# A recurrent attention and a squared-ReLU layer on one core: attention in two stretches of small products, and three passes summed in one bank

## The chip, the core and the metric

The kernel runs on one core of a Trainium2 chip. Five engines work side by side, each from its own queue in order: TensorE (PE in the profile: matrix products into PSUM, with its weight loads shown as PEld), VectorE (DVE), ScalarE (ACT), GpSimd (POOL) and SyncE (SP), which here issues all DMA transfers. PSUM has eight banks of 128 partitions x 512 fp32 values; a sum of products builds up in one bank and is read from there by VectorE or ScalarE. The metric is the device time of one execution in microseconds.

## What is computed

```python
# q, k, v, alpha: (4, 8, 768, 48); batch, heads, sequence, head size
for t in range(S):
    state = alpha[:, :, t, :, None] * state + einsum('bhd,bhe->bhde', k[:, :, t], v[:, :, t])
    y[:, :, t] = einsum('bhd,bhde->bhe', q[:, :, t], state)
x = y.transpose(0, 2, 1, 3).reshape(3072, 384)
h = maximum(x @ w_in, 0.0)          # w_in  (384, 2048)
out = h * h @ w_out                 # w_out (2048, 384)
```

All in fp32; the weights arrive as 64-bit floats and are converted on the chip.

## The kernel before

**Blocks, groups, pairs.** The sequence is cut into chunks of 128 positions; one chunk of one batch entry is a block (24 in all, numbered chunk first). Four blocks are a group (512 tokens; six groups, 0 to 5). Attention is worked on in pairs of blocks, the dense layers in groups. While TensorE does the dense layers of group g, the attention of group g + 1 is threaded between their products.

**Attention of a pair.** Logarithms of alpha (`pair_ln`) are summed along the chunk by a product with a triangle of ones (`cs`), and their exponentials scale k and q (`eb`, `ei`, `pair_mk`, `pair_mq`). Then come four kinds of small products, which use 64 rows of the array each so that several run at a time: `turn` (L672) transposes k and q in halves of 64 positions (16 transposes a block, 64 rows by 128 columns) into two banks, and `turned_copied` (L686) copies them to SBUF; `pair_scores` (L545, 64 products into two banks) multiplies k and q of the same half, and `pair_masked` on VectorE (L563) copies the causal part out; `pair_sums` (L569, up to 64 products into two banks) multiplies k and v; `pair_states` (L587) adds these to the running state in three VectorE instructions (L596, L603, L604); and `y_first`, `y_second` (L623, L640, 96 and 32 products into two banks) make the output. `y_second` writes from the other half of the rows into banks that `y_first` has written, and so its first product waits for an instruction on POOL's queue (L636) that itself waits for the end of `y_first`. `ev` (L697, L714) copies y to the place of the next layer's input.

**Where these stand.** `PLAN` (L1155) gives offsets in units of dense work, `attention` (L1172) turns them into events, and `weave` (L1213) emits every event that is due before the next unit. A unit of 1 is about 1.3 us of TensorE. For a step with start t, `turn` of both new blocks stands at one place, `ga` at a second and `gb` at a third. `ga` (L653) emits the scores and masks of pair n and `y_first` of the pair before it; `gb` (L662) emits the sums of pair n, `y_second` of the pair before, and the states of n. The numbers in `AT` (L19) set all starts, due times, split sizes and the engines of some copies. The work on the first four blocks is written out by hand in the string `first` (L1139); there k and q are transposed by 128x128 transposes (`turned`, L416).

**Dense layers in three passes.** From group 1 on, a product x w is made of parts that TensorE multiplies at its faster fp32r rate. With E = 2^-12, x = a / E + l and w = E (b + lw), where a and b are rounded to fp32r. Then

x w = (1 + E) (a b + l lw) + (a - l)(lw - E b).

`split_to` (L808) makes a on ScalarE (L809) and l on VectorE (L810); `diff_to` (L814) makes a - l on VectorE (recorded at L747). The weights' parts are made by `cast_w`, `rest_w` and `diff_w` (L759 to L791), stored to DRAM and streamed back from there in each group; `room` caps how many tiles of them are asked for at a time, in a pool of 25 buffers. Per piece j of 128 of the 2048 columns, `in_x` (L842) does the first two passes into one bank; then the factor is applied in one of two ways, by the letter in `kinds` for j modulo 4. With "D", ScalarE copies E times the bank to SBUF (L849), the third pass is added to the same bank (`in_y`, L853), VectorE adds the copy (L856, recorded at L747) and then takes maximum and square in one instruction (L863). With "A", ScalarE multiplies the bank in place (L851), the third pass is added, and ScalarE does ReLU and square (L868, L872). The third pass follows `lag` pieces behind, the activation `post` pieces behind. `layer_in` lists these units.

**The second layer** works the same way on h * h (`split_h`, `diff_h`, three parts a piece). In groups 2 to 4 the output is made transposed (`turned_x`, `turned_y`, L993 and L1009), with ScalarE multiplying the bank in place between the passes (L1005) and VectorE transposing it at the end (L1022). Group 5 and the last k1 of the eight weight pieces in group 1 (k0 in group 0) use `out_x` and `out_y` (L941, L965); between the passes E times the bank goes to or into the output tile (L956, L961), and VectorE adds the bank at the end (L979, recorded at L747). The other pieces of groups 0 and 1 use plain fp32 products (`out_plain`, L929), which leave two TensorE records each. The first layer of group 0 is plain too (`ffn_in`, L1083).

Of the kernel before, what the change touches and what calls it, by code (L numbers as in the profile page):

```python
# [9 lines left out]
FP32 = mybir.dt.float32  # L10
# [3 lines left out]
ALU = mybir.AluOpType  # L14
# [4 lines left out]
AT = {'pad': 1, 'lag': 2, 'joined': 0, 'tc': 0.02, 'u0': 2, 'evs': 0.55, 'lead': 6, 'post': 2, 'w_first': (38.96, 41.47, 110.86), 'wstep': 2.64, 'w_in_at': 0.78, 'w_in_by': 3.53, 'room1': 24, 'room': 27, 's0': 3, 'ahead': 12, 'late': 23, 'xs': 0.23, 'g0': (3.39, 20.49, 26.97), 'sc0': (2.38, 2.19, 2.43), 'g1': (3.89, 18.11, 27.72), 'g': (3.4, 16.07), 'g1x': 51.78, 'gx': 47.62, 'g0x': 56.0, 'k0': 2, 'h0': 15, 'k1': 5, 'h1': 1, 'h1by': 1, 'evs0': 0.17, 'tp': 'DDAD', 'tp1': 'AADD', 'split': 8, 'o0': (41.33, 43.5), 'o1': (), 'o2': (18.91, 14.16, 27.32, 25.44, 44.09, 46.91), 'str1': 19.63, 'ga': 9.84, 'gb': 13.76, 'osb': 'DD', 'hia': 16}  # L19
# [6 lines left out]
def kernel(  # L26
# [406 lines left out]
    VECTOR = ('k0', )  # L433
# [6 lines left out]
    def qc(n):  # L440
        (copied if n < GB else turned_copied)("q", n)

    def kc(n):
        (copied if n < GB else turned_copied)("k", n)
# [203 lines left out]
    def turn_and_copy(m):  # L648
        turn(m)
        kc(m)  # L650
        qc(m)
# [34 lines left out]
    def turned_copied(x, n):  # L686
        t = blk[n][f"{x}s"] = work(f"{x}s", 2 if x == "k" else 4)
        for h in range(2):
            nc.scalar.copy(out=t[:, :, HALF[h]], in_=blk[n]["T"][h][:, "kq".index(x)])
# [40 lines left out]
    NEAR = 1.0 - 2.0**-13  # L730
    acc = {}
# [47 lines left out]
    def diff_w(w, p):  # L779
# [4 lines left out]
            out=d, in0=b, scalar=-E, in1=l, op0=ALU.mult, op1=ALU.add  # L784
# [29 lines left out]
    def diff_to(d, a, l):  # L814
        combine(((d, a.bitcast(FP32), ALU.subtract, l.bitcast(FP32)),))
# [11 lines left out]
    def diff_x(g):  # L827
        x_parts["d"] = raw_r("xd")
        diff_to(*(flat(x_parts[k]) for k in "dal"))
# [12 lines left out]
    def in_x(j):  # L842
        acc["h", j] = ps_ffn.tile([128, GB * C], FP32, tag="att", name="h")
        in_passes(j, "b", "a", True, False)
        in_passes(j, "l", "l", False, True)
        x = acc["h", j]
        if kinds[0][j % 4] == "D":
            hid[j] = two_k("hid")
            nc.scalar.activation(out=hid[j], in_=x, func=AF.Copy, scale=E)  # L849
        else:  # L850
            nc.scalar.activation(out=x, in_=x, func=AF.Copy, scale=1.0 + E)  # L851
# [6 lines left out]
    kinds = [""]  # L858

    def in_post(j):  # L860
        if kinds[0][j % 4] == "D":
            h = hid[j]
            nc.vector.scalar_tensor_tensor(  # L863
                out=h, in0=h, scalar=0.0, in1=h, op0=ALU.max, op1=ALU.mult
            )
            return
        h = hid[j] = two_k("hid")
        nc.scalar.activation(out=h, in_=acc.pop(("h", j)), func=AF.Relu)  # L868
        if kinds[0][j % 4] == "M":
            combine(((h, h, ALU.mult, h),))  # L870
        else:
            nc.scalar.activation(out=h, in_=h, func=AF.Square)  # L872
# [20 lines left out]
    def split_h(n, i):  # L893
# [8 lines left out]
        split_to(a, l, hid.pop(n))  # L902
        h_parts[n] = a, l

    def diff_h(n):
        h_diff[n] = two_k("hd", FP32R)
        diff_to(h_diff[n], *h_parts[n])
# [33 lines left out]
    def out_x(n, first, g):  # L941
        p, jj = divmod(n, 2)
        a, l = h_parts.pop(n)
        for t in range(GB):
# [3 lines left out]
            of_tile(t, l, mixed(here["l", "o", p], jj), stop=n == NJ - 1)  # L948
            if n == NJ - 1:
                x = unmixed(acc[t])  # L950
                if first and AT["osb"][g] == "A":
                    x = acc[t][:, 0:DM]
                    nc.scalar.activation(out=x, in_=x, func=AF.Copy, scale=1.0 + E)
                elif first:
                    o = out_tile(t).rearrange("a (q c) -> a q c", c=DM // 128)
                    nc.vector.scalar_tensor_tensor(  # L956
                        out=o, in0=x, scalar=E, in1=o, op0=ALU.mult, op1=ALU.add
                    )
                else:
                    o = new_out(t).rearrange("a (q c) -> a q c", c=DM // 128)  # L960
                    nc.scalar.activation(out=o, in_=x, func=AF.Copy, scale=E)  # L961
# [3 lines left out]
    def out_y(g, ps, t, last):  # L965
# [5 lines left out]
        if last:  # L971
            o = out_tile(t)
# [3 lines left out]
            for i in range(parts):  # L976
                qs = slice(i * 128 // parts, (i + 1) * 128 // parts)
                cols = slice(i * DM // parts, (i + 1) * DM // parts)
                combine(((o[:, qs], x[:, qs], ALU.add, o[:, qs]),))  # L979
# [7 lines left out]
    TURNED = (2, 3, 4)  # L987
# [5 lines left out]
    def turned_x(n):  # L993
        p, jj = divmod(n, 2)
        a, l = h_parts.pop(n)
        for c in range(NM):
            if n == 0:
                acc[c] = ps_ffn.tile([128, GB * C], FP32, tag="att", name="o")
            for w, x in (("b", a), ("l", l)):
                nc.tensor.matmul(  # L1000
                    out=acc[c], lhsT=by_parts(here[w, "o", p], jj, c), rhs=x,
                    start=n == 0 and w == "b", stop=n == NJ - 1 and w == "l", skip_group_check=True,
                )
            if n == NJ - 1:
                nc.scalar.activation(out=acc[c], in_=acc[c], func=AF.Copy, scale=1.0 + E)  # L1005
# [77 lines left out]
    def ffn_in(g, j, cols=slice(0, GB * C)):  # L1083
# [14 lines left out]
        nc.scalar.activation(out=hid[j][:, cols], in_=r, func=AF.Square)  # L1098
# [34 lines left out]
    for x in "stky":  # L1133
# [6 lines left out]
        load1v warm0 warm0 load0v ln0 cs0 ln1 warm0 ei0 eb0 cs1 warm0 mq0 mk0 load2a  # L1140
        weights0 qT0 load3a kT0 eb1 mq1 ei1 warm0 mk1 kc0 qc0 kT1 qT1 kc1 sc0 qc1 kv0 sc1
        lt1 ln2 load2k cs2 am1 load2q lc1 kv1 gt1 am0 warm0 ln3 load3q warm0 us0 cs3 ei2
        first0 us1 ya0 yb0 lt0 eb2 eb3 ei3 st1 mk2 mq2 ea00 load3k kT2 kc2 warm0 lc0 load2v
        mq3 qT2 ed02 gy0 weights1 load3v middle0 lt2 st0 lt3 mk3 qT3 kT3 warm0 warm0 lc2
        qc2 sc2 kc3 qc3 ed01 second0 first1 ea03 load4q middle1 kv2 load4k weights2 am2 us2
        sc3 kv3 am3 us3 gk3 lc3 load4a second1 ha0 weights3 ya2 yb2 ea20 ed21 ed22 ha1 ed23
        first2 middle2 ha3 st3 ha2 load4v hb1 hb0 weights4 st2
    """
    for word in first.split():
# [6 lines left out]
        (-0.48, "pair_ln"),  # L1156
        (-0.27, "pair_sp"),
        (2.08, "cs0 cs1 eb0 ei0"),
        (2.23, "eb1 ei1"),
        (3.01, "pair_bl"),  # L1160
        (3.13, "pair_mk"),
        (4.43, "pair_mq"),
        (5.99, "pair_br"),
        (6.75, "turn"),
        (7.02, "kc0 qc0"),
        (7.36, "kc1 qc1"),
        (9.56, "ga"),
        (10.29, "gb"),
    )
    JOINED = AT["joined"]  # L1170

    def attention(pairs, scale):  # L1172

        out = []
        for t, n0, after, *last in pairs:
# [146 lines left out]
```

## Time and profile before

| what | value |
|---|---|
| three timed runs | 514.6, 513.85, 514.68 us (median 514.6) |
| profiled execution, its own time | 514.06 us |
| its span | 512.3 us |
| TensorE clock granted | 1.00 throughout |
| TensorE products busy | 505.1 us, 5164 records |
| VectorE busy | 371.5 us, 550 instructions |
| ScalarE busy | 304.3 us, 611 instructions |
| DMA | 102.72 MB, mean 201 GB/s |
| dense layers of groups 1, 2, 3, 4, 5 begin at | 123.8, 210.8, 289.4, 368.0, 442.6 us |
| last product ends | 508.6 us |

Times in the profile count from the start of the span, which is a little shorter than the device time. A row of a group gives line, engine, operation, output and inputs, shape, count, busy time and mean duration of one; behind the second bar stands how long the engine was idle just before these instructions and which instruction ended most of that. Products overlap in the array, so that the starts of records, and not their durations, tell how fast TensorE goes on. The chain of waits is followed back from the last instruction, at each step to what released it.

### The profile page before, as it was taken

To read this page: it belongs to the slowest core of one execution; us is meant where nothing else is said; L and a number is where in the kernel's file an instruction comes from. 1 tells how busy PE (TensorE), PEld (TensorE's weight loads), DVE (VectorE), ACT (ScalarE), POOL (GpSimd) and SP (SyncE) were. 2 spreads that over 40 slices of the span, in tenths; PEclk is the share of its full clock that TensorE was granted. 3 is DMA by queue.
4 is the path that set the end of the run, shared out by engine and by line. 5 is a ranking of instruction groups with operands and counts; after the bars stand their busy time and mean duration, and the time that the engine had idled before them with its cause. 6 is when DMAs were issued, how large, how long until landed. Compare 5 with 4: busy or idle time off the path is not lost.

```text
span 512.3 us, 12578 instructions
## 1 busy us (share of the span) xinstructions
PE 505.1 (99%) x5164; PEld 402.5 (79%) x5164; DVE 371.5 (73%) x550; ACT 304.3 (59%) x611; POOL 5.6 (1%) x27
## 2 busy tenths in 40 slices
PE   8999999999999999999999999999999999999997
PEld 6684456669887679988888888888888888888996
DVE  3898879978879957687795388694477685466951
ACT  4689893766988586375863165954165863154520
POOL 4000000000000000000000000000000000000000
PEclk9999999999999999999999999999999999999999
DMA  9999669254978886896877877876874645889201
GB/s 185 217 268 263 196 170 260 51 154 151 289 225 233 217 175 170 291 332 181 177 202 210 275 219 189 185 216 167 267 215 135 201 113 146 276 282 363 91 1 63
DMA packets 144521, 102.72 MB, mean 201 GB/s; under 512 B 116296, under 2 KB 117960, under 8 KB 144464
## 3 DMA queue, kind: packets, MB, share of 16 engines
q1 hardware_dynamic: 144464, 101.91, 70.8%
q8 instruction: 41, 0.67, 0.5%
q14 instruction: 16, 0.13, 0.1%
HBM read 84.57 MB, written 17.33 MB: 199 GB/s over the span
## 4 chain that ended last, share of the span: by engine, by line
PE 94%; DVE 2%; SPq 2%; DMA 1%; issue 0%; ACT 0%; DVEq 0%; POOLq 0%
PE h L834 33%; PE o L913 22%; PE o L1000 13%; PE h L1090 8%; PE o L1012 6%; PE y L465 5%; PE T L681 2%; PE sc L553 2%; PE kv L580 2%; SPq L134 2%; DMA a_lent<-in_alpha_dram 1%; PE cs L327 1%; PE cs L330 1%; PE cs L331 1%; DVE am L494 0%
## 5 line engine op out<-in xcount | busy, mean ns | idle before, releaser
L849 ACT ACTIVATE hid<-h 128x512 f32<-128x512 f32 x56 | 33.3, 595 | 66.2 <-PE h L834 65.6
L834 PE MATMUL h<-xa,wb 128*128 128x512 f32 x240 | 67.7, 391 | 0.0
L834 PE MATMUL h<-xl,wl 128*128 128x512 f32 x240 | 67.6, 390 | 0.0
L834 PE MATMUL h<-xd,wd 128*128 128x512 f32 x240 | 67.5, 396 | 0.0
L714 ACT COPY x<-y 32x256 f32<-32x256 f32 (+2 forms) x137 | 48.6, 366 | 22.8 <-PE y L465 20.5
L747 DVE TENSOR_TENSOR hid<-h,hid 128x512 f32<-128x512 f32 x56 | 38.6, 689 | 28.0 <-PE h L834 25.4
L834 PEld LDWEIGHTS h<-xl,wl 128*128 128x128 f32 x240 | 45.1, 188 | 9.6
L834 PEld LDWEIGHTS h<-xa,wb 128*128 128x128 f32 x240 | 44.9, 188 | 9.5
L834 PEld LDWEIGHTS h<-xd,wd 128*128 128x128 f32 x240 | 44.0, 188 | 8.9
L913 PE MATMUL o<-w_out,hid 128*128 128x384 f32 x144 | 49.0, 492 | 0.0
L1090 PE MATMUL h<-x,w_in 128*128 128x512 f32 (+1 forms) x120 | 42.4, 509 | 0.0
L863 DVE SCALAR_TENSOR_TENSOR hid<-hid 128x512 f32<-128x512 f32 x56 | 38.7, 692 | 1.8
L913 PEld LDWEIGHTS o<-w_out,hid 128*128 128x128 f32 x144 | 26.6, 190 | 17.0
L809 ACT ACTIVATE ha<-hid 128x512 fp32r<-128x512 f32 x42 | 26.2, 638 | 19.1 <-DVE hx L810 11.7
L1090 PEld LDWEIGHTS h<-x,w_in 128*128 128x128 f32 x120 | 22.6, 190 | 17.2 <-issue 14.6
L810 DVE SCALAR_TENSOR_TENSOR hl<-ha,hid 128x512 fp32r<-128x512 f32 x42 | 28.8, 686 | 7.4 <-ACT ha L809 7.3
L1012 PE MATMUL o<-hd,wd 128*128 128x512 f32 x144 | 33.4, 391 | 0.0
L1012 PEld LDWEIGHTS o<-hd,wd 128*128 128x128 f32 x144 | 26.8, 188 | 6.1 <-ACT o L1005 0.6
L747 DVE TENSOR_TENSOR hd<-ha,hl 128x512 fp32r<-128x512 f32 x42 | 29.1, 692 | 2.4
L810 DVE SCALAR_TENSOR_TENSOR hx<-hx,hid 128x512 fp32r<-128x512 f32 x36 | 24.7, 685 | 7.9 <-ACT hx L809 7.9
L851 ACT ACTIVATE h<-h 128x512 f32<-128x512 f32 x24 | 14.0, 584 | 24.7 <-PE h L834 24.6
L1000 PE MATMUL o<-hx,wb 128*128 128x512 f32 x72 | 28.4, 394 | 0.0
(135 smaller groups left out, 945.8 us busy)
## 6 DMA issues: line engine op xcount, KB each, us to landing
wd<-do SPq DMA_DIRECT2D x37, 384.0 KB, 4.2
wl<-lo SPq DMA_DIRECT2D x34, 384.0 KB, 3.8
wl<-li SPq DMA_DIRECT2D x32, 384.0 KB, 4.4
wd<-di SPq DMA_DIRECT2D x32, 384.0 KB, 5.8
raw<-in_moe_w_in_dram SPq DMA_DIRECT2D x8, 768.0 KB
raw<-in_moe_w_out_dram SPq DMA_DIRECT2D x8, 768.0 KB
v_in<-in_v_dram SPq DMA_DIRECT2D x24, 192.0 KB, 3.8
a_in<-in_alpha_dram SPq DMA_DIRECT2D x22, 192.0 KB, 4.0
```

The source lines that it names most:

```text
L465: ins = nc.tensor.matmul(out=ys[e][64 * half : 64 * half + D + G * e, m % 2, p // 2, t], lhsT=lhsT, rhs=rhs, start=(half, e) not in seen, ...
L714: copy(out=x[kk][to : to + m, t : t + 2], in_=blk[n]["y"][e][r : r + m, :, p // 2],)
L747: nc.vector.tensor_tensor(out=o, in0=x, in1=z, op=op)
L809: nc.scalar.activation(out=a, in_=x, func=AF.Copy, scale=NEAR * E)
L810: nc.vector.scalar_tensor_tensor(out=l, in0=a.bitcast(FP32), scalar=-1.0 / E, in1=x, op0=ALU.mult, op1=ALU.add)
L834: nc.tensor.matmul(out=acc["h", j], lhsT=here[w, "i", p][:, kk, jj * 128 : (jj + 1) * 128], rhs=x_parts[x][:, kk], start=start and kk == 0 ...
L849: nc.scalar.activation(out=hid[j], in_=x, func=AF.Copy, scale=E)
L863: nc.vector.scalar_tensor_tensor(out=h, in0=h, scalar=0.0, in1=h, op0=ALU.max, op1=ALU.mult)
L913: nc.tensor.matmul(out=acc[t][:, 0:DM], lhsT=lhs[:, t * C : (t + 1) * C], rhs=rhs, start=start, stop=stop, skip_group_check=True,)
L1000: nc.tensor.matmul(out=acc[c], lhsT=by_parts(here[w, "o", p], jj, c), rhs=x, start=n == 0 and w == "b", stop=n == NJ - 1 and w == "l", ski ...
L1012: nc.tensor.matmul(out=acc[c], lhsT=by_parts(here["d", "o", p], n % 2, c), rhs=h_diff[n], start=False, stop=last and n == NJ - 1, skip_gro ...
L1090: nc.tensor.matmul(out=ps, lhsT=w[:, kk, c0 : c0 + 128], rhs=xT[g][kk][:, cols], start=(kk == 0), stop=(kk == KM - 1),)
```

## The change

**Factor.** The third part of x and of h is now made as a - x E / (1 + E), that is E (a - l) / (1 + E), and that of w as (w_l / E - b), so that the third product is 1 / (1 + E) of what it was. All three passes then add up in one bank to x w / (1 + E). The factor 1 + E of the first layer stands in the scale of the ReLU; that of the second layer stands in the square of h. The copies and the multiplications between the passes are gone (L849, L851, L956, L961, L1005), and so is the "D" way. A letter now names only the engine of the square: "V" is VectorE, "A" is ScalarE. Since the difference now reads h itself, h is kept until then. Where a whole output is made by three passes, VectorE copies it from the bank instead of adding.

**Attention.** A step now emits two stretches. `stretch_a` emits, for pair n, scores, masks and sums, then the transposes of the first block of the pair ahead, then the states of n and the copies of what was transposed. `stretch_b` emits `y_first` of the same pair n, the transposes of the second block ahead, `y_second`, and the copies. A step is prepared one pair further ahead, so that group 0 has a first step with transposes alone; loads of k, v and q are issued at the stretches.

**Numbers.** `AT` is new in nearly all entries (among them lag 2 to 1, post 2 to 1, k1 5 to 6, pad 1 to 9, the letters of `kinds`), the hand-written order `first` is permuted, with four of its warm-up products (`warm0`) left out and the engines of two copies of y (`ea03`, `ed02`) swapped, k and q of blocks 1 to 3 are transposed by halves, and VectorE takes the copies of k0, k2, q0, q1 and q2 (k0 alone before).

```diff
-AT = {'pad': 1, 'lag': 2, ... 'room1': 24, 'room': 27, 's0': 3, 'ahead': 12, ... 'k0': 2, 'h0': 15, 'k1': 5, ... 'tp': 'DDAD', 'tp1': 'AADD', ... 'ga': 9.84, 'gb': 13.76, 'osb': 'DD', 'hia': 16}
+AT = {'turned': (2, 3, 4), 'ht': '123', 'vc': ['k0', 'k2', 'q0', 'q1', 'q2'], 'pad': 9, 'lag': 1, ... 'post': 1, ... 'room1': 23, 'room': 25, 's0': 2, 'ahead': 11, ... 'k0': 2, 'h0': 16, 'k1': 6, ... 'tp': 'AVVA', 'tp1': 'AVVV', ... 'ga': 8.09, 'gb': 12.66, 'hia': 8}
...
+        if str(n) in AT["ht"]:
+            if "T" not in blk[n]:
+                blk[n]["T"] = [bank(n, "T", (2, NP, 64)) for _ in range(2)]
+            for p in range(NP):
+                for h in range(2):
+                    marks["t", n] = nc.tensor.transpose(
+                        out=blk[n]["T"][h][:, "kq".index(x), p, :],
+                        in_=rows[HALF[h], 128 * p : 128 * (p + 1)], identity=ident[HALF[h], HALF[h]],
+                    )
+            return
...
-    def ga(a, n, t):
-        if t is not None and JOINED:
-            turn_and_copy(t)
+    def stretch_a(n, t):
         if n is not None:
             pair_scores(n)
             pair_masked(n)
-        if a is not None:
-            y_first(a)
-
-    def gb(a, n, t):
-        if t is not None and JOINED:
-            turn_and_copy(t + 1)
-        if n is not None:
             pair_sums(n)
-        if a is not None:
-            y_second(a)
+        if t is not None:
+            turn(t)
         if n is not None:
             pair_states(n)
+        if t is not None:
+            kc(t)
+            qc(t)
+
+    def stretch_b(n, t):
+        if n is not None:
+            y_first(n)
+        if t is not None:
+            turn(t + 1)
+        if n is not None:
+            y_second(n)
+        if t is not None:
+            kc(t + 1)
+            qc(t + 1)
...
-            out=d, in0=b, scalar=-E, in1=l, op0=ALU.mult, op1=ALU.add
+            out=d, in0=l, scalar=1.0 / E, in1=b, op0=ALU.mult, op1=ALU.subtract
...
-    def diff_to(d, a, l):
-        combine(((d, a.bitcast(FP32), ALU.subtract, l.bitcast(FP32)),))
+    def diff_to(d, a, x):
+        nc.vector.scalar_tensor_tensor(
+            out=d, in0=x, scalar=-E / WHOLE, in1=a.bitcast(FP32), op0=ALU.mult, op1=ALU.add
+        )
...
-        in_passes(j, "l", "l", False, True)
-        x = acc["h", j]
-        if kinds[0][j % 4] == "D":
-            hid[j] = two_k("hid")
-            nc.scalar.activation(out=hid[j], in_=x, func=AF.Copy, scale=E)
-        else:
-            nc.scalar.activation(out=x, in_=x, func=AF.Copy, scale=1.0 + E)
+        in_passes(j, "l", "l", False, False)
 
     def in_y(j):
         in_passes(j, "d", "d", False, True)
-        if kinds[0][j % 4] == "D":
-            combine(((hid[j], acc.pop(("h", j)), ALU.add, hid[j]),))
+
+    def squared(h, kind, scale):
+        if kind == "V":
+            nc.vector.scalar_tensor_tensor(
+                out=h, in0=h, scalar=scale, in1=h, op0=ALU.mult, op1=ALU.mult
+            )
+        else:
+            nc.scalar.activation(out=h, in_=h, func=AF.Square, scale=scale**0.5)
...
         h = hid[j] = two_k("hid")
-        nc.scalar.activation(out=h, in_=acc.pop(("h", j)), func=AF.Relu)
-        if kinds[0][j % 4] == "M":
-            combine(((h, h, ALU.mult, h),))
-        else:
-            nc.scalar.activation(out=h, in_=h, func=AF.Square)
+        nc.scalar.activation(out=h, in_=acc.pop(("h", j)), func=AF.Relu, scale=WHOLE)
+        squared(h, kinds[0][j % 4], WHOLE if j >= plain_part[0] else 1.0)
...
-            if n == NJ - 1:
-                nc.scalar.activation(out=acc[c], in_=acc[c], func=AF.Copy, scale=1.0 + E)
...
-    steps0 = [(GB, False), (GB + 2, True), (GB + 4, True, True)]
-    if JOINED:
-        steps0.insert(0, (GB - 2, False))
+    steps0 = [(GB - 2, True), (GB,), (GB + 2,)]
```

More of the change, by code (lines that the diff above doesn't have):

```diff
@@ L730 @@
     NEAR = 1.0 - 2.0**-13
+    WHOLE = 1.0 + E
     acc = {}
@@ L947, in out_x @@
             of_tile(t, a, mixed(here["b", "o", p], jj), start=n == first)
-            of_tile(t, l, mixed(here["l", "o", p], jj), stop=n == NJ - 1)
-            if n == NJ - 1:
[L950 to L961, printed above, removed]
+            of_tile(t, l, mixed(here["l", "o", p], jj))
         if jj:
@@ L978, in out_y @@
                 cols = slice(i * DM // parts, (i + 1) * DM // parts)
-                combine(((o[:, qs], x[:, qs], ALU.add, o[:, qs]),))
+                if alone:
+                    nc.vector.tensor_copy(out=o[:, qs], in_=x[:, qs])
+                else:
+                    combine(((o[:, qs], x[:, qs], ALU.add, o[:, qs]),))
                 store(g, t, out_tile(t)[:, cols], cols)
```

123 lines of the change are left out of this document (53 added, 70 removed).

## The prediction

> **What bounds the kernel now.** I read the page's busy shares and chain first, then the chain in order of time, then TensorE's timeline where small products interrupt large ones, then the costliest groups.
>
> ```profile
> PE 505.1 (99%) x5164; PEld 402.5 (79%) x5164; DVE 371.5 (73%) x550; ACT 304.3 (59%) x611; POOL 5.6 (1%) x27
> PE 94%; DVE 2%; SPq 2%; DMA 1%; issue 0%; ACT 0%; DVEq 0%; POOLq 0%
> ```
>
> The chain is TensorE for 94% of the span; in order of time it leaves TensorE only before 30 us (loads, then VectorE) and after 508.6. From 30 us, time is saved only by shortening TensorE's stream, and lost only by making TensorE wait. Around a stretch of transposes (columns: start, us, engine, line, operation, operands):
>
> ```profile
> 138.22 0.84 PE L834 MATMUL h<-xl,wl 128*128 128x512 f32 x3
> 138.99 0.46 PE L681 MATMUL T<-ident,k_in 64*128 64x64 f32 x8
> 139.29 0.42 PE L681 MATMUL T<-ident,q_in 64*128 64x64 f32 x8
> 139.54 0.42 PE L681 MATMUL T<-ident,k_in 64*128 64x64 f32 x8
> 139.79 0.42 PE L681 MATMUL T<-ident,q_in 64*128 64x64 f32 x8
> 140.14 0.98 PE L834 MATMUL h<-xd,wd 128*128 128x512 f32 x3
> 140.96 0.86 PE L834 MATMUL h<-xa,wb 128*128 128x512 f32 x3
> 141.65 0.85 PE L834 MATMUL h<-xl,wl 128*128 128x512 f32 x3
> ```
>
> Read the starts. Undisturbed triples come every 0.685 us. From 138.22 + 0.685 = 138.905 to 141.65 - 2 x 0.685 = 140.28 is 1.375 us for 32 transposes, which run at 0.25 us per 8, so 1.00 us: the visit costs 0.375 beyond its work. The stretch of 64 scores at 144.49 costs 0.315 the same way (1.295 between the large products, less 64 scores in 0.98, the step from 74.05 to 75.03 where sums follow scores). Two more rows show another change of form:
>
> ```profile
> 12.18 0.57 PE L485 MATMUL sckv<-qs,ks 48*64 48x64 f32 x24
> 12.69 0.43 PE L407 MATMUL cs<-ident,b_wide 32*128 32x32 f32 x4
> ```
>
> The last score starts at 12.54 and the first 32-row transpose at 12.69, though scores follow each other at 0.015.
>
> The groups that the change touches on the other engines:
>
> ```profile
> L849 ACT ACTIVATE hid<-h 128x512 f32<-128x512 f32 x56 | 33.3, 595 | 66.2 <-PE h L834 65.6
> L747 DVE TENSOR_TENSOR hid<-h,hid 128x512 f32<-128x512 f32 x56 | 38.6, 689 | 28.0 <-PE h L834 25.4
> L863 DVE SCALAR_TENSOR_TENSOR hid<-hid 128x512 f32<-128x512 f32 x56 | 38.7, 692 | 1.8
> L851 ACT ACTIVATE h<-h 128x512 f32<-128x512 f32 x24 | 14.0, 584 | 24.7 <-PE h L834 24.6
> L1012 PEld LDWEIGHTS o<-hd,wd 128*128 128x128 f32 x144 | 26.8, 188 | 6.1 <-ACT o L1005 0.6
> L872 ACT ACTIVATE hid<-hid 128x512 f32<-128x512 f32 x24 | 15.2, 632 | 0.8
> ```
>
> They wait for TensorE; hardly any of TensorE's idle time is put down to them.
>
> **The change, part by part.** The sum starts from the profiled execution's 514.06 us (span 512.3), 0.54 below the median 514.6 of the three timed runs.
>
> *Factor in the third pass and the ReLU.* Removed: ScalarE 33.3 + 14.0 (L849, L851), 4.7 (L1005), 1.6 (L961); VectorE 38.6 + 38.7 (L747 on hid, L863), 3.9 (L956). Added: 56 more ReLUs x 0.612 = 34.3 and 12 more squares x 0.632 = 7.6 on ScalarE; 44 squares x 0.692 = 30.4 on VectorE. Net ScalarE -12, VectorE -51. All of it lies beside TensorE, so the time gains nothing by it, except the 0.6 that weight loads waited for L1005: **-0.3** (0 to -0.6). The split differences keep one VectorE instruction each (686 for 692 ns). hid now lives until its difference is made, so with 22 buffers the first such difference of the second layer waits for the first out product; TensorE's next three inputs are ready by then, which covers it. The third pass one piece behind instead of two: its ScalarE partner is gone, nothing.
>
> *One more w_out piece in three passes in group 1 (k1 5 to 6).* Sixteen plain records go (4 tiles x 2 halves x 2): 10.52 us for 32 in the chain, so 5.26. Added 24 products, 15.48 us for 88, so 4.22. **-1.04**, all on the path. Preparing it was done anyway; only its kept copies and loads move.
>
> *Fewer stretches.* After 30 us the trace has 33 visits to small products: 10 of transposes, 10 begun by scores, 9 by sums, 4 of y products alone. After the change each of 10 pairs has two, and the first two blocks' transposes, which fall into one unit boundary, add one: 21. Twelve fewer at 0.315 to 0.375: **-4.2** (-3.8 to -4.5).
>
> *New changes of form inside a stretch.* Sums to transposes in the first, y to transposes to y in the second: 27 over nine pairs (the last pair has no transposes). No such pair of neighbours is in the trace. Scores to sums in one form cost nothing seen (one end, 0). Scores to 32-row transposes left 0.149 instead of 0.015, and the transposes' first eight took 0.05 longer (0.30 for 0.25): 0.18 (other end; 4.9 in all). In that row rows and columns both change, here only the columns, so I take two thirds, 0.12: **+3.2**.
>
> *y_second behind y_first.* It waits for a POOL instruction. At 17.12 y products took until 19.03 where 96 at 0.45 per 32 and one change make 1.5: 0.4 of wait. Sixteen transposes (0.50) cover that in the new stretch, except for the last pair: **+0.4** (0 to 0.5).
>
> *Start.* ScalarE's logarithm of blocks 2 and 3 gates the chain until 15.7 (DMA 9.38 + 6.30); the second of those loads goes two places earlier (two loads of 192 KB at the stretch's 213 GB/s: 1.8 us earlier), but both v loads go behind it, and the same 15 loads must land before blocks 2 and 3 are complete. VectorE, which gates the y products at 28.28, gets 1.4 us of copies for block 2 (four at about 0.35 by the halves of L438's 0.69). Eight more pads (0.29 each by L270's pair) lie in the wait for the first load; two warm products are left out there and two further on. **+0.3** (-1.5 to +2).
>
> *Queues.* Loads of q, k and v move to the stretches on SP's queue; each is used more than five units (6 us) later against 3.8 to 4.6 us to landing. The weights' buffers are 25 in both, so lower room numbers start no transfer later. POOL keeps its one instruction per pair. Nothing.
>
> Sum: 514.06 - 0.3 - 1.04 - 4.2 + 3.2 + 0.4 + 0.3 = **512.4 us**.
>
> **Rivals.**
>
> *Inner changes are free:* 512.4 - 3.2 = 509.2, with a better start 508. For it: 48x48, 48x64 and 64x48 products alternate inside y and sums without a gap. Against: every change of form in the trace shows one.
>
> *Inner changes cost the full 0.18:* 512.4 + 1.7 = 514.1, no change. For it: the gap is 0.148 to 0.155 whatever forms meet (scores to 128 rows, 32-row transposes to 128, 64-row transposes to 128). [...]
>
> *TensorE waits for VectorE and banks (slower):* scores, sums and transposes now hold six of eight PSUM banks at once, and two h sums the rest; the next h sum needs a bank 0.68 us after the transposes end, when the masks (1.36 us, begun 1.5 us before that end) must have freed one. That holds while VectorE starts the masks less than about 0.8 us late. Before, it started 0.05 to 3.1 us late (scores end 254.68, mask 257.80). If ten pairs wait 0.45 each: 516.9. Above 0.32 each it is slower. Against: VectorE has 51 us less, and in the second stage of each group the masks now stand ahead of the splits.
>
> *The start loses 2 us:* 514.1 to 514.4.
>
> **How the numbers follow.** Chances: the forecast (511 to 513.4) 0.34; free 0.25; full price 0.17; waits 0.17; start 0.07. 0.2% of the median, 1.03 us, is about what a measurement can tell from no change: faster means under 513.57. Faster: 0.34 + 0.25 and some 0.03 of the last three, 0.62. Same: most of full price and start, 0.18. Slower: waits and the tails, 0.20. The range, 508.6 to 517.0, takes in free and waits to their centres; the forecast's own is 511 to 513.4.
>
> **What would show it.** Twenty-one stretches; the gap from the last sum or y product to the first transpose (0.015, 0.09 or 0.15 us) sets the price. No L849 or L851, 80 ReLUs, 44 squares on VectorE. Second-layer plain records 128. Wrong if waits of TensorE for masks, states or banks reach 3 us in sum, or if large products begin for good more than 1.5 us from 29.96.

## The result, and the profile after

| | before | after |
|---|---|---|
| median (range) of six runs each | 514.64 us (513.85 to 515.99) | 518.82 us (518.61 to 519.17) |
| profiled execution, its own time | 514.06 us | 518.65 us |
| its span | 512.3 us | 516.9 us |
| dense layers begin for good, last product ends | 30.03, 508.59 us | 35.38, 513.32 us |

The ratio is 1.0075, with a 95% interval from 1.0056 to 1.0094. The change made the kernel 4.2 us slower; 512.4 us was forecast, with a range up to 517.0, and the time lies above it. The last row of the table says where to look: the part from the first lasting run of large products to the last product takes 477.94 us instead of 478.56, so it became 0.6 us shorter, but it begins 5.35 us later.

The page of the kernel after (engines' busy time, granted clock, chain by engine, and two groups of other engines):

```profile
PE 510.1 (99%) x5204; PEld 411.2 (80%) x5204; DVE 322.7 (62%) x488; ACT 289.2 (56%) x584; POOL 5.5 (1%) x27
...
PEclk9979999999999999999999999999999999999999
...
PE 98%; DVE 1%; issue 0%; POOL 0%; DVEq 0%; POOLq 0%
...
L876 ACT ACTIVATE hid<-h 128x512 f32<-128x512 f32 x80 | 47.7, 603 | 96.8 <-PE h L848 58.6
L866 DVE SCALAR_TENSOR_TENSOR hid<-hid 128x512 f32<-128x512 f32 x44 | 30.3, 690 | 68.6 <-ACT hid L876 68.5
```

VectorE and ScalarE do less, as forecast, and still wait for TensorE. TensorE's share of the chain rose from 94% to 98%. That looks like a better filled engine; but it lies at the start, where loads led the chain before and TensorE itself leads it now. Of the 4 points (some 20 us), 9.6 us are pads (products of 8 columns ahead of the first attention work) and warm-up products (256 columns), which compute nothing that is read; the rest is attention of the first blocks, part of it at a lower clock: the third slice has a granted clock of 7 tenths. A row of the chain in order of time (columns: start, length, engine, operation and line, count) shows the pads:

```profile
4.02 3.64 PE pad L270 x18
```

And TensorE's timeline, first of before, then of after (start, length, operation; in brackets the idle time just before and what ended it):

```profile
3.81 0.43 PE L270 MATMUL pad<-s 128*128 128x8 f32 x2
4.10 1.50 PE L260 MATMUL warm<-s 128*128 128x256 f32 x4
5.44 0.81 PE L327 MATMUL cs<-a_in,causal 128*128 128x384 f32 x2
...
7.29 0.91 PE L327 MATMUL cs<-a_in,causal 128*128 128x384 f32 x2 [0.61 <-ACT a_in L291]
```

```profile
3.82 3.85 PE L270 MATMUL pad<-s 128*128 128x8 f32 x18
7.52 1.63 PE L327 MATMUL cs<-a_in,causal 128*128 128x384 f32 x2
...
10.64 1.49 PE L327 MATMUL cs<-a_in,causal 128*128 128x384 f32 x2
...
25.71 0.69 PE L425 MATMUL T<-ident,k_in 64*128 64x64 f32 x8 [1.43 <-DVE k_in L358]
```

Look at the first `cs` in the timeline of before: it has no bracket. It waited for nothing but TensorE's own queue, since ScalarE had made its input (L291, 0.52 us from 3.60 on) by 4.12 us. So whatever is put in front of it delays it. After the change the first `cs` is 2.1 us later and the second 3.35 us later, and the products themselves take 1.63 us where they took 0.81: the full clock, granted at 4.91 us before, now comes at 12.08. (These times are from the clock's own records, which begin with that grant; the 1.00 throughout in the table of before holds from there on. Ahead of the grant half clock is read from the starts: the warm-up records of before follow each other by 0.43 us ahead of it and by 0.21 behind it.)

Later TensorE waits 1.43 us for VectorE at 25.71. By the next view (windows of 4 us of the kernel after: window, length, busy time and count of TensorE's products, of its weight loads, of VectorE, ScalarE and POOL, granted clock, DMA share, GB/s) the clock is then halved:

```profile
24.00:28.00 4.00, 2.57 (x50) 1.98 (x48) 3.96 (x8) 0.65 (x2) 0.00 (x0) 0.72 0.73 149
28.00:32.00 4.00, 4.00 (x104) 3.75 (x103) 2.51 (x9) 2.94 (x9) 0.00 (x0) 0.50 1.07 325
```

In the clock's own records it is half from 25.73 to 32.56 us. Before the change it was full in all of these windows. The table of TensorE's waits after the change has three entries, all ahead of the dense work: this one, 1.1 us for POOL at the very start, and 0.5 for VectorE at 13.94. So the slower rival of the prediction, waits for masks and banks, did not occur in this execution.

### The profile page after: what moved, and what is told of

Its sections match the earlier page's. It is cut to its first block, busy times and chain, and to the rows that moved or that the text cites. A ratio compares the mean times of both kernels' runs of the same rounds, so it can differ in the third digit from the quotient of the medians.

```text
span 516.9 us, 12503 instructions
## 1 busy us (share of the span) xinstructions
PE 510.1 (99%) x5204; PEld 411.2 (80%) x5204; DVE 322.7 (62%) x488; ACT 289.2 (56%) x584; POOL 5.5 (1%) x27
## 4 chain that ended last, share of the span: by engine, by line
PE 98%; DVE 1%; issue 0%; POOL 0%; DVEq 0%; POOLq 0%
PE h L848 32%; PE o L918 21%; PE o L996 13%; PE h L1084 8%; PE o L1006 6%; PE y L475 5%; PE T L691 2%; PE sc L563 2%; PE kv L590 2%; PE cs L327 1%; PE warm L260 1%; PE pad L270 1%; PE sckv L522 1%; PE sckv L495 1%; PE cs L330 1%; PE T L425 1%
## 5 line engine op out<-in xcount | busy, mean ns | idle before, releaser
L876 ACT ACTIVATE hid<-h 128x512 f32<-128x512 f32 x80 | 47.7, 603 | 96.8 <-PE h L848 58.6
L866 DVE SCALAR_TENSOR_TENSOR hid<-hid 128x512 f32<-128x512 f32 x44 | 30.3, 690 | 68.6 <-ACT hid L876 68.5
L725 ACT COPY x<-y 32x256 f32<-32x256 f32 (+3 forms) x138 | 50.0, 364 | 4.0 <-DVE x L725 0.8
L918 PE MATMUL o<-w_out,hid 128*128 128x384 f32 x128 | 43.4, 491 | 0.0
L918 PEld LDWEIGHTS o<-w_out,hid 128*128 128x128 f32 x128 | 23.8, 190 | 15.5 <-issue 0.5
L827 DVE SCALAR_TENSOR_TENSOR hd<-hid,ha 128x512 fp32r<-128x512 f32 x42 | 28.7, 684 | 10.7 <-PE o L996 9.7
L700 ACT COPY ks<-T 128x256 f32<-128x256 f32 x44 | 14.2, 375 | 36.6 <-PE T L691 32.7
L822 DVE SCALAR_TENSOR_TENSOR hx<-hx,hid 128x512 fp32r<-128x512 f32 x38 | 26.0, 684 | 6.7 <-ACT hx L821 6.7
L996 PE MATMUL o<-hx,wl 128*128 128x512 f32 x72 | 28.1, 390 | 0.0
```

The source lines that it names most:

```text
L725: copy(out=x[kk][to : to + m, t : t + 2], in_=blk[n]["y"][e][r : r + m, :, p // 2],)
L822: nc.vector.scalar_tensor_tensor(out=l, in0=a.bitcast(FP32), scalar=-1.0 / E, in1=x, op0=ALU.mult, op1=ALU.add)
L827: nc.vector.scalar_tensor_tensor(out=d, in0=x, scalar=-E / WHOLE, in1=a.bitcast(FP32), op0=ALU.mult, op1=ALU.add)
L866: nc.vector.scalar_tensor_tensor(out=h, in0=h, scalar=scale, in1=h, op0=ALU.mult, op1=ALU.mult)
L918: nc.tensor.matmul(out=acc[t][:, 0:DM], lhsT=lhs[:, t * C : (t + 1) * C], rhs=rhs, start=start, stop=stop, skip_group_check=True,)
L996: nc.tensor.matmul(out=acc[c], lhsT=by_parts(here[w, "o", p], jj, c), rhs=x, start=n == 0 and w == "b", stop=False, skip_group_check=True,)
```

## Experiments on the start

Three kernels ask what in the start is late. The first takes the change and puts the start of before in it (the string `first`, one pad, k and q of blocks 1 to 3 transposed whole, `k0` alone on VectorE).

```diff
-AT = {..., 'ht': '123', 'vc': ['k0', 'k2', 'q0', 'q1', 'q2'], 'pad': 9, ...
+AT = {..., 'ht': '', 'vc': ['k0'], 'pad': 1, ...
-        ln0 cs0 ln1 warm0 warm0 ei0 load2a weights0 cs1 eb0 ei1 mk0 mq0 kT0 load3a warm0
...
+        load1v warm0 warm0 load0v ln0 cs0 ln1 warm0 ei0 eb0 cs1 warm0 mq0 mk0 load2a
...
```

> The changed kernel with the start of the kernel before: its hand-written order, one pad, blocks 1 to 3 transposed 128x128, VectorE copying k0 alone. The changed kernel begins its dense work for good at 35.4 us, the kernel before at 30.0. Theory A (the whole loss lies in the start; the dense part gained 0.65 us): dense work from about 30.0, 518.7 - 5.4 = 513.3 us. Rival (TensorE's dense part loses to waits for masks or banks, and the later start only moves them): above 516.

The second undoes only the pads:

```diff
-AT = {..., 'pad': 9, ...
+AT = {..., 'pad': 1, ...
```

> The changed kernel with one pad product instead of nine, nothing else. Theory A1 (the pads, which take 3.64 us at half clock, hold the first sum of logarithms and the full clock back): the first cs at about 5.4 instead of 7.5, full clock before 8 instead of at 12.1, dense work from 31 to 32.5, 514.5 to 516. Rival A2 (the order and the copies on VectorE make the start late, and the pads lie in a wait): dense work no earlier than 34.5, 517.8 or more.

The third puts the nine pads into the kernel before:

```diff
-AT = {'pad': 1, ...
+AT = {'pad': 9, ...
```

> The kernel before with nine pads instead of one, nothing else. A1: the first cs at 7.5, full clock only after 8, dense work from 32 to 34, 516.5 to 518.5. A2: the loads of blocks 2 and 3 set the start anyway, dense work within 1 us of 30.0, 514.4 to 515.6.

Measured, beside 514.58 us for the kernel before on the same chip: 515.44 us with the old start (ratio 1.0018, 1.0009 to 1.0028), 515.59 with one pad (1.0022, 1.0012 to 1.0031), 518.18 for before with nine pads (1.0082, 1.0051 to 1.0114). Taking the pads out gives 3.2 us (518.82 to 515.59); putting them into before costs 3.6. The pads alone account for about three quarters of the loss. The second and third kernels came out as A1 said, but for the first `cs` (4.24 us for 5.4, and 9.36 for 7.5); the first kernel lies between theory A and its rival. In the profiled execution of before with nine pads, which took 521.2 us, TensorE stood still twice for 4.6 us in sum behind "issue", which the last experiment below takes up. The 3.6 is the median of its four executions, and some of it may be such waits.

With one pad TensorE's wait for k, and the half clock after it (0.50 from 24 to 28 us), are still there (timeline of the change with one pad):

```profile
22.54 0.47 PE L425 MATMUL T<-ident,k_in 64*128 64x64 f32 x8 [1.43 <-DVE k_in L358]
...
32.30 1.99 PE L1084 MATMUL h<-x,w_in 128*128 128x256 f32 x8
```

The first `cs` starts at 4.24 us instead of 7.52, and everything behind it is 3.0 to 3.4 us earlier than after the change; large products begin for good at 32.30 instead of 35.31. With the old start they begin at 30.28, 0.3 us later than before, and the clock stays full (1.00 from 20 to 32 us); that kernel is hardly faster than the one with one pad, and 1.3 of the 2.0 us go to later waits of TensorE behind "issue" (taken up in the last experiment).

**What the half clock costs.** Four warm-up products of 256 columns (`warm0`, two records each) are put into the wait for VectorE:

```diff
-        ... kc2 mk3 warm0 kT3 ...
+        ... kc2 mk3 warm0 warm0 warm0 warm0 warm0 kT3 ...
```

> e2 (changed kernel, one pad; 515.6) with four more warm-up products where TensorE waits 1.8 us for VectorE's scaling of k of block 3. They compute nothing that is read. Theory (that idle time halves the granted clock from 23.4 to 30.2 us, and the half clock makes dense work begin at 32.3 instead of 30): no half clock, dense work from about 30.5, 513.8 to 514.5. Rival (VectorE's chain of copies and masks sets the start, whatever the clock): dense work from 31.8 or later, 515.1 or more.

Measured: 514.55 us beside 514.54 for before (1.0002, 0.9991 to 1.0014), 1.0 us less than with one pad alone and just above the theory's range. The wait is gone, the clock stays full (1.00 from 20 to 36 us), and large products begin for good at 31.27 us (timeline):

```profile
20.52 2.43 PE L260 MATMUL warm<-s 128*128 128x256 f32 x10
22.88 0.46 PE L425 MATMUL T<-ident,k_in 64*128 64x64 f32 x8
...
31.27 3.10 PE L1084 MATMUL h<-x,w_in 128*128 128x256 f32 x13
```

The transposes even start 0.34 us later than with one pad alone, and yet the large products start 1.03 earlier: that is the clock's doing in these two executions (0.50 from 24 to 28 us with one pad alone, 1.00 here). The 1.0 us in the medians is less sure to be the clock's alone. With one pad not every execution was halved for 6.83 us: the mean clock was 0.992 or 0.993 in seven (median 515.66 us) and 0.997 to 1.0 in three (514.94 to 515.39), so that within this kernel the half clock goes with some 0.3 us. What else the four products gain was not separated.

Eight products of 8 columns, as the pads are, in the same place, ask whether any product does it:

```diff
-        ... kc2 mk3 warm0 kT3 ...
+        ... kc2 mk3 warm0 small0 kT3 ...
```

> e2 (changed kernel, one pad; 515.6) with eight 8-column products, like the pads, in the place where e8 has four warm-up products of 256 columns. They compute nothing that is read. Theory (products of 8 columns don't keep the granted clock up, as the nine pads didn't bring it up for 3.64 us): half clock from about 23.4 as in e2, 515.4 to 516. Rival (any product keeps it up; the pads at the start merely came too early): no half clock, 514.3 to 515.

Measured: 516.06 us beside 514.26 (1.0035, 1.0022 to 1.0048). The products of 8 columns did not keep the clock up (windows of 4 us, columns as above):

```profile
20.00:24.00 4.00, 4.00 (x76) 3.72 (x71) 3.60 (x8) 1.01 (x3) 0.00 (x0) 1.00 0.95 254
24.00:28.00 4.00, 4.00 (x109) 3.73 (x109) 2.85 (x8) 2.55 (x8) 0.00 (x0) 0.52 0.99 256
```

TensorE is busy for the whole of the first window by these records, and the clock is still halved at 24.16 us. So "busy" in the profile was not what kept the clock here: in the same place products of 256 columns kept it and products of 8 did not. (Eight of the ten executions had a mean clock of 0.992 or 0.993, median 516.1 us; the other two had 0.997 and took 514.51 and 514.72.) It fits the nine pads, too. They took 0.41 us a pad (18 records from 3.82 to 7.52), where the eight in the gap, at full clock, took 0.22 (16 records from 20.90 to 22.68), and with them the full clock came at 12.08 us (after) and 10.64 (before with nine pads); in the eleven traces with one pad it came between 4.33 and 7.25. So 3.7 us of products of 8 columns did not bring it up. After the change a wait of 1.43 us, among narrow products, was followed by 6.83 us at half clock. In the clock's own records every stretch between two changes is a whole multiple of 3.41 us (after the change 13.65, 6.83 and 484.69 us, which are 4, 2 and 142 of them).

**What is left of the late start.** With one pad and the warm products the dense work still begins 1.3 us later than before (31.27 for 29.96). One suspect were the copies that VectorE took over:

```diff
-AT = {..., 'vc': ['k0', 'k2', 'q0', 'q1', 'q2'], 'pad': 1, ...
+AT = {..., 'vc': ['k0'], 'pad': 1, ...
```

> e8 (changed kernel, one pad, four more warm-up products; 514.55) with VectorE copying k0 alone, as before the change; ScalarE takes the copies of k2, q0, q1 and q2. Theory (VectorE's 1.4 us of copies for block 2 and 1.3 for blocks 0 and 1 are what is left of the late start, 31.8 against 30.5 in e1): dense work from 30.5 to 31, 513.3 to 514. Rival (ScalarE is as full at the start and the order decides): 514.3 or more.

Measured: 514.68 us beside 514.26 (1.0009, 1.0000 to 1.0018), dense work from 31.42 us. It is not the copies. The order of the string, and the transposes of blocks 1 to 3 by halves, are what remains of the change there; which step is the late one was not separated.

## Experiments on the stretches

The prediction counted stretches and put 0.12 us on a change of form inside one. Two other orders of the same work, both with the old start, change the number of forms that meet. (A form, as counted here, is the rows and columns of a product as the timeline has them, with 48 and 64 taken as one, since those products follow each other at 0.015 us: 64x64, 64x128 for the transposes, 128x128 for the large products.) In the first, scores move to the other stretch, next to the products of the same form:

```diff
     def stretch_a(n, t):
-            pair_scores(n)
-            pair_masked(n)
             pair_sums(n)
             turn(t)
+            turn(t + 1)
             pair_states(n)
...
     def stretch_b(n, t):
             y_first(n)
-            turn(t + 1)
+            pair_scores(t)
             y_second(n)
+            pair_masked(t)
```

> e1 (changed kernel, old start; 515.4) with other neighbours in the two stretches: the first holds sums, then the transposes of both blocks ahead; the second holds y_first, then the scores of the pair ahead (transposed a stretch before), then y_second. The same products; five changes of form a pair instead of seven, and the masks are made a whole step before they are read. Theory (each change of form costs TensorE about 0.17 us wherever it stands): 18 fewer in nine pairs, -3.1, so 512.3 us (511.5 to 513). Rival (six banks are held again, four of them by transposes until ScalarE has copied them, and TensorE waits for a bank): 515 or more. Rival (changes inside a stretch are free after all): 515.4.

Measured: 527.7 us beside 514.54 (1.0263, 1.0247 to 1.0280), 12 us slower than the change with the old start, where the theory had 512.3; the rival has the direction right and, as will be seen, 3.2 us of the cause. There are 17 changes of form fewer in the dense part (52 for 69: the pairs save 18, the scores put ahead of the first pair add one), yet TensorE stands still (its waits: total, times, longest; then its timeline at one of them):

```profile
PE y L475 <- issue: 6.8, 3, 3.9
PE sc L563 <- ACT qs L699: 3.2, 1, 3.2
PE h L847 <- issue: 2.1, 1, 2.1
```

```profile
239.60 0.51 PE L475 MATMUL y<-am,v_in 64*48 64x64 f32 x22
244.00 0.41 PE L475 MATMUL y<-am,v_in 64*48 64x64 f32 x8 [3.89 <-issue]
```

It waits for no semaphore there. In the trace a transfer of the instruction queue runs from 241.45 to 242.57 us, and TensorE goes on 1.4 us after its end: I read this as having run out of instructions, and the last experiment takes it up. The account nearly closes: 7.6 us more of "issue" than with the old start (8.9 for 1.3), 3.2 for the first scores, which wait for ScalarE's copies at 57.69 us, and two periods at half clock after such waits (56.4 to 63.2 and 244.1 to 247.6 us), which at half speed lose up to 5.1; together up to 15.9, less 17 changes at 0.148 = 2.5, makes up to 13.4. Measured between the two profiles is 12.9 to the end of the last product (522.58 for 509.66).

In the second order the transposes go ahead of `y_first`, so that nothing lies between it and `y_second`:

```diff
     def stretch_b(n, t):
+        if t is not None:
+            turn(t + 1)
         if n is not None:
             y_first(n)
-        if t is not None:
-            turn(t + 1)
         if n is not None:
             y_second(n)
```

> e1 with the second stretch reordered: transposes, y_first, y_second, so that nothing stands between y_first and y_second. One change of form fewer a pair (-0.17 x 9 = -1.5), but y_second now waits for the POOL instruction behind y_first. Theory (that wait is 0.4 us, as at the start of the kernel before): +3.6 - 1.5, so 517.5 us (516.8 to 518.2). Rival (the wait is short): 513.9 to 515.

Measured: 516.67 us (1.0047, 1.0032 to 1.0062), 1.2 us slower than with the transposes between: the theory's direction, at a little over half of its 2.1. The groups 2 and 3 take 79.24 and 79.19 us instead of 78.79 and 78.74. From the last product of `y_first` to the first of `y_second` TensorE now stands 0.345 us, the wait for POOL's instruction, where 0.015 is the step between two such products. Two pairs a group at 0.33, less one change of form each at 0.15, is 0.36; measured is 0.45.

**The price of a change of form** can be read in the kernel after itself. These are one pair's rows in its timeline:

```profile
262.36 0.68 PE L475 MATMUL y<-am,v_in 64*48 64x64 f32 x31
262.97 0.46 PE L691 MATMUL T<-ident,k_in 64*128 64x64 f32 x8
...
263.62 0.69 PE L475 MATMUL y<-am,v_in 64*48 64x64 f32 x32
264.24 0.50 PE L996 MATMUL o<-hx,wb 128*128 128x512 f32 x1
```

From the last start of a product of one form to the first of the next it is 0.149 to 0.150 us from 64 to 128 columns (18 times in the dense part), 0.153 to 0.155 back (9 times), and 0.148 to 0.149 from 64x64 products to the large ones. The first eight transposes also take 0.30 us from start to start of the eights (262.97 to 263.27), against the 0.25 of eights further on in a visit before the change. It makes no difference that here only columns change.

## Experiments on the factor and on k1

The factor alone, in the kernel before, with its order, its numbers and its stretches (the letters of `kinds` follow the new meaning):

```diff
-... 'tp': 'DDAD', 'tp1': 'AADD', ...
+... 'tp': 'VVAV', 'tp1': 'AAVV', ...
...
-        in_passes(j, "l", "l", False, True)
-        x = acc["h", j]
-        if kinds[0][j % 4] == "D":
...
+        in_passes(j, "l", "l", False, False)
...
+        nc.scalar.activation(out=h, in_=acc.pop(("h", j)), func=AF.Relu, scale=WHOLE)
```

> The kernel before with the first part of the change alone: the three passes in one bank, the factor in the ReLU and the square; attention, start, piece counts and all due times as before; the squares that were VectorE's stay there. Forecast's step: -0.3 (0 to -0.6), so 514.0 to 514.6, with ScalarE and VectorE some 45 us and 50 us less busy together with no effect on TensorE. Rival (their load did cost TensorE waits in the dense part): 512.5 or less.

Measured: 514.56 us beside 514.58 (1.0006, 0.9996 to 1.0016). VectorE's busy time falls from 371.5 to 324.0 us and ScalarE's from 304.3 to 284.7 (page of this kernel):

```profile
PE 505.9 (98%) x5164; PEld 402.9 (78%) x5164; DVE 324.0 (63%) x486; ACT 284.7 (55%) x574; POOL 5.5 (1%) x27
```

67 us of work less on two engines (47.5 and 19.6, where the expectation had 50 and 45), and the time does not move: they had waited for TensorE all along. The 0.3 us that the prediction took for L1005 is too small to be told from nothing here.

The sixth piece in three passes, alone in the kernel before:

```diff
-... 'k0': 2, 'h0': 15, 'k1': 5, ...
+... 'k0': 2, 'h0': 15, 'k1': 6, ...
```

> The kernel before with one more w_out piece in three passes in group 1 (k1 6 instead of 5), nothing else. Forecast's step: -1.04, so 513.5 us. Rival (the parts of that piece aren't made in time with the old due times, and TensorE waits): 514.4 or more.

Measured: 521.23 us beside 514.54 (1.0152, 1.0113 to 1.0191). Group 1 takes 93.13 us instead of 86.85. TensorE waits 1.7 us for instructions there, 0.9 for VectorE's L810, and 1.9 for ScalarE (timeline):

```profile
183.98 0.27 PE L681 MATMUL T<-ident,k_in 64*128 64x64 f32 x1 [1.38 <-ACT x L714]
184.76 0.69 PE L681 MATMUL T<-ident,k_in 64*128 64x64 f32 x7 [0.51 <-ACT x L714]
```

The due times of before don't suit it. TensorE's transposes wait for ScalarE's copies of y (L714), and between these copies ScalarE has three splits of h to make (L809, 1.67 us from 181.87 on), which come behind them, at 185.94, in the kernel before. The clock is halved behind the wait (184.7 to 188.2 us, and 195.0 to 198.4 behind the wait for instructions). This run does not test the 1.04 us of the prediction in a kernel whose due times fit, and after the change TensorE has no such wait; but it does say that this part is not free of the rest of `AT`.

## An experiment on the instructions

The change with the old start has two waits behind "issue", 0.58 us at 83.13 and 0.68 at 117.81, which after the change are not there. If they come from the position of a block of instructions, they must move when instructions are put in ahead. Two warm-up products go in before 83 us, which are eight instructions (two records each, and a weight load with each):

```diff
-        ... mk3 qT3 kT3 warm0 warm0 lc2
+        ... mk3 qT3 warm0 kT3 warm0 warm0 lc2
...
-        ... second1 ha0 weights3 ya2 yb2 ...
+        ... second1 ha0 weights3 warm0 ya2 yb2 ...
```

> e1 (changed kernel, old start; 515.4) with two more warm-up products where TensorE waits at the start, which moves every later instruction of TensorE by eight places within the blocks of 256 in which they are fetched. Theory (the two waits of 0.6 and 0.7 us in e1's second stretches of group 0, which nothing in the profile explains and which come with an instruction transfer just before their end, are fetches of instructions, and hang on where a block ends): those waits change or go, others may come; if they go, 514.1 us (1.3 less). Rival (they belong to the work there): both waits stay within 0.1 us of their length, 515.4.

Measured: 515.18 us beside 514.26 (1.0017, 1.0008 to 1.0027), as with the old start. The waits are still there and have moved (timeline, first with the old start, then with the two warm products):

```profile
81.99 0.56 PE L475 MATMUL y<-am,v_in 64*48 64x64 f32 x21
83.13 0.44 PE L475 MATMUL y<-am,v_in 64*48 64x64 f32 x11 [0.58 <-issue]
...
117.81 0.34 PE L475 MATMUL y<-am,v_in 64*48 64x64 f32 x7 [0.68 <-issue]
```

```profile
81.72 0.48 PE L475 MATMUL y<-am,v_in 64*48 64x64 f32 x17
82.98 0.46 PE L475 MATMUL y<-am,v_in 64*48 64x64 f32 x15 [0.79 <-issue]
...
118.01 0.45 PE L475 MATMUL y<-am,v_in 64*48 64x64 f32 x11 [1.04 <-issue]
```

21 products ahead of the first wait became 17, and 7 behind the second became 11: four small products, which with their weight loads are eight instructions, as many as were put in. So the wait hangs on the position in the instruction stream and not on the data. The shift moved it within the stretch and not out of it, and it grew; a larger shift was not tried. The other traces bear it out. Number TensorE's own instructions as a trace has them in order, from 0: products, weight loads and the few others on its queue. Waits of TensorE behind "issue" occur in eight of the experiments' kernels, sixteen in all, and each of the sixteen ends at a number that is 193 or 194 more than a multiple of 256. Here they are 1986 and 2754, the same with and without the shift.

## Why the prediction was wrong

The step of the prediction that failed is **Start**: "Eight more pads (0.29 each by L270's pair) lie in the wait for the first load", with +0.3 us in the sum. Two things in it were wrong. There was no wait for the pads to lie in: the first `cs` had no idle time before it in the trace of before, and the only wait nearby, 0.61 us for ScalarE, stood before the second. And a pad costs 0.41 us and not 0.29, with the full clock coming at 12.08 us where it came at 4.91 before. The pads alone are worth 3.2 us. The prediction also let the load of blocks 2 and 3 gate the start; after the change no load stands in the chain, which is TensorE's own from 1.10 us on but for two waits for VectorE. And it gave the four warm products less no price of their own; but TensorE's 1.43 us of idle time before 25.71 lies where they could have stood, and filling it gives 1.0 us. By medians the loss is closed: 518.82 less 3.23 for the pads is 515.59, less 1.04 for the wait and the half clock behind it is 514.55, which is the time of before. Within that a start still 1.3 us late stands against a dense part 0.7 us shorter (477.86 us with the warm products, 478.56 before). The rest is about what lies between the two profiled executions, 514.55 and 514.06, of which that of before lies 0.5 under its kernel's median.

The rival "the start loses 2 us" was the right mechanism at less than half of its size, with a chance of 0.07. The prediction's own last condition, large products for good more than 1.5 us from 29.96, is what came: 35.31.

*New changes of form* was undersized: 0.12 us each was forecast, for 27. The rival "full price" was right that they cost what every other change costs. Groups 2 and 3, which have the same products in both kernels, measure it. Per group of two pairs, two stretches fewer at the prediction's 0.315 to 0.375 should give 0.69 and six inner changes take it back; measured is +0.16 and +0.18 us (78.79 for 78.63, 78.75 for 78.57), so six cost 0.86 and one 0.14 to 0.145. By 27 that is 3.9 us in place of 3.2. In the timeline, too, 64x64 to 64x128 leaves the same gap as the other changes, 0.149 us. Counted so, the change gains next to nothing by joining stretches: 4.2 us against 3.9. Twelve stretches fewer save 24 changes of form at their ends, and 27 are new inside: 66 before, 69 after.

*Fewer stretches*: 33 visits in the dense part became 21, as counted. Their price was not measured by itself, and the 0.14 above rests on it.

*y_second*: right. The transposes cover the wait for POOL, and for the last pair, which has none, the gap is 0.346 us, where 0.4 was taken. Without that cover the kernel is 1.2 us slower.

*The factor*: right, nothing on TensorE's path; 80 ReLUs, 44 squares on VectorE and 128 plain records are as forecast.

*The dense part as a whole* was to gain 1.9 us (0.3, 1.04 and 4.2, less 3.2 and 0.4) and gained 0.6. The price of the inner changes explains 0.7 of the 1.3 missing, and the 0.3 for L1005 isn't seen. The rest, some 0.3, is not placed; it may lie in the 1.04 for the sixth piece, which no run measured by itself without waits.

*Waits for masks and banks*, the slower rival: not there. TensorE's table of waits after the change has nothing behind 30 us.

## What to carry to other kernels

Before filling a wait at the start, look for the bracket: a product with no idle time before it has no room in front of it, and every filler there is paid in full, here at half clock (0.41 us a pad). In a real wait products of 256 columns paid here and products of 8 columns did not. Before joining stretches of small products, count the changes of form and not the stretches alone, and see that the stretch isn't so long that instructions run out (192 products in a row came with 8.9 us of waits behind "issue" here). And a rising share of TensorE in the chain is no gain until one has read which of its products compute something.

## What the runs showed of the hardware

**Instructions came in blocks of 16 KB, and small products outran them.** The page's queue for them, in the kernel after:

```profile
q8 instruction: 41, 0.67, 0.5%
```

41 transfers of 0.67 MB in sum are 16 KB each, and 5204 records of products with a weight load each, in 41 blocks, are 254 instructions to a block, if the queue serves TensorE alone. The sixteen waits at every 256th instruction, above, say the same. A stretch of small products, with 0.015 us from product to product, uses up such a block in about 2 us (an estimate: 127 products at 0.015). TensorE went on 1.2 to 1.4 us after the end of a transfer (80.91 to 81.89 and then 83.13, 115.2 to 116.5 and then 117.81 with the old start; 241.45 to 242.57 and then 244.00 with the scores moved), and so it is in fifteen of the sixteen waits; in the other it was 1.8. The waits were 0.4 to 3.9 us; with 192 products in a row they came to 8.9 us in one execution.

**Products of 8 columns did not hold the clock, nor bring it up**, though the profile counts TensorE as busy: with eight of them in the gap it was halved at 24.16 us, and with nine pads the full clock came at 12.08 and 10.64. Some waits were followed by half clock: waits of 1.4 to 3.9 us went with 3.4 or 6.8 us at half clock (from 25.7 us after the change, from 184.7 with the sixth piece alone, from 244.1 with the scores moved). But a wait of 2.90 us before 196.30 in the kernel before with nine pads, and one of 2.12 us before 329.80 with the scores moved, left it full. The stretches between changes of the clock were multiples of 3.41 us, so where a wait falls between two such steps may have decided; that is a guess, and no run varied it by itself.

**A change of form took 0.148 to 0.155 us from start to start**, where small products of one form follow each other at 0.015. That held from one small form to another and from a small form to the large products, and joining 64x64 products to 64x128 transposes was such a change, at 0.149 to 0.150.
